# A fused linear-attention and token-mixing kernel: 128-token chunks on full 128-row operands with a block-diagonal state, whole-batch loads, and an explicit order that assigns every PSUM bank

## The chip, the cores and the metric

The kernel runs on one core of a Trainium2 chip. The metric is the device time of one execution in microseconds (us), as a median over several executions. A profile is a recording of one of them; its "span" is about 1.7 us shorter than the time of the same run (113.8 us against 115.53 us in a run of the kernel before). "Slow" here means over 1.5% above the fastest run of the same kernel.

## The reference, cut to what matters

```python
# q, k, v: (batch 4, heads 8, seq 768, head_dim 64), float32
gamma = 1.0 - 2.0 ** (-5.0 - np.arange(H))
for t in range(S):                                   # linear attention with decay
    state = gamma * state + einsum('bhd,bhe->bhde', k[:, :, t], v[:, :, t])
    y[:, :, t] = scale * einsum('bhd,bhde->bhe', q[:, :, t], state)
x = y as (B, S, 512)
wq, wk = x @ w_q, x @ w_k                            # 512 -> 64
W_tok = scale * einsum('bsd,btd->bst', wq, wk)
mixed = einsum('bst,btd->bsd', W_tok, x)
out = maximum(mixed, 0) @ w_out                      # (4, 768, 512) float32
```

Both kernels process it in 12 pairs of two 128-token chunks, three pairs to a batch. Two words are used throughout: a "filler" is a matmul on zeros whose result nobody reads, issued to keep TensorE busy; an "eviction" is a copy of a result from PSUM, where TensorE writes, to SBUF. The decay is folded into k and q when they are cast to bf16. Inside a chunk, scores are computed, masked and multiplied with v ("intra"); what came earlier enters through a 64x64 state per head ("inter"). The second half then works on the 256 tokens of a pair.

Of the kernel before, what the change touches and what calls it, by code (L numbers as in the profile page):

```python
# [9 lines left out]
FP32 = mybir.dt.float32  # L10
# [5 lines left out]

ORDER = """
fill.80 ck.0:V trk.0 cq.0:V ekT.0:A trq.0 cv.0:V fill.2 eqT.0:V
st.0 es.0.0:A sc.0.0 X.0 eat.0.0:V es.0.1:A sc.0.1 ck.1:P ia.0.0
eat.0.1:V cq.1:P Y.0 trk.1 fill.6 ekT.1:A ia.0.1 ex.0:V cv.1:P  # L20
trq.1 eqT.1:A xt.0 st.1 sc.1.0 exT.0:V ck.2:P es.1.0:A eat.1.0:V
X.1 es.1.1:A sc.1.1 cq.2:P trk.2 eat.1.1:V ia.1.0 ekT.2:V Y.1
ia.1.1 cv.2:A ex.1:V trq.2 st.2 fill.4 eqT.2:V xt.1 es.2.0:A
W:V sc.2.0 exT.1:A X.2 wqk.0 eat.2.0:V wqk.1 WO:A ew.0:V
sc.2.1 ew.1:V ia.2.0 eat.2.1:V ck.3:P Y.2 ia.2.1 ex.2:A cq.3:P
trk.3 xt.2 ekT.3:A fill.4 exT.2:V cv.3:A wqk.2 trq.3 ew.2:A
st.3 eqT.3:V zm.0 ck.4:P es.3.0:A ez.0:A X.3 sc.3.0 es.3.1:A
mx.0 eat.3.0:V r.0.1:A cq.4:P trk.4 r.0.0:A sc.3.1 ekT.4:A ia.3.0
eat.3.1:V mx.1 Y.3 r.1.0:A pj.0.0 cv.4:P r.1.1:A trq.4 fill.4
eo.0.0:A st.4 eqT.4:V ia.3.1 ck.5:P pj.0.1 ex.3:A es.4.0:V sc.4.0  # L30
eo.0.1:A X.4 eat.4.0:V xt.3 es.4.1:V cq.5:P trk.5 ekT.5:A exT.3:V
pj.1.0 sc.4.1 eo.1.0:A cv.5:P trq.5 eat.4.1:V ia.4.0 mx.2 eqT.5:A
YS.4 ia.4.1 es.5.0:A ck.6:P r.2.0:A ex.4:V wqk.3 trk.6 r.2.1:A
sc.5.0 pj.1.1 ew.3:A eat.5.0:V cq.6:P eo.1.1:A X.5 ekT.6:V ia.5.0
sc.5.1 cv.6:A xt.4 eat.5.1:V trq.6 pj.2.0 exT.4:A eqT.6:V ck.7:P
YS.5 eo.2.0:A sc.6.0 es.6.0:A ia.5.1 eat.6.0:V wqk.4 cq.7:P ex.5:A
pj.2.1 ew.4:A trk.7 eo.2.1:V xt.5 ekT.7:V sc.6.1 X.6 exT.5:V
cv.7:A eat.6.1:V trq.7 ia.6.0 eqT.7:A wqk.5 ck.8:P es.6.1:A sc.7.0
ew.5:V YS.6 eat.7.0:V es.7.0:A ia.6.1 zm.1 ex.6:A cq.8:P sc.7.1
ez.1:V X.7 eat.7.1:V trk.8 es.7.1:A xt.6 ekT.8:V cv.8:A ia.7.0  # L40
trq.8 exT.6:V Y.7 st.8 eqT.8:V mx.3 es.8.0:A ia.7.1 ck.9:P
r.3.1:A r.3.0:V sc.8.0 ex.7:V wqk.6 eat.8.0:V pj.3.0 ew.6:A cq.9:P
trk.9 eo.3.0:A pj.3.1 ekT.9:V X.8 eo.3.1:A cv.9:P mx.4 sc.8.1
r.4.0:A r.4.1:V trq.9 eat.8.1:V pj.4.0 eqT.9:A ck.10:P ia.8.0 eo.4.0:V
mx.5 YS.8 r.5.1:A r.5.0:V sc.9.0 ia.8.1 es.9.0:V pj.4.1 cq.10:P
ex.8:V trk.10 eo.4.1:A eat.9.0:V pj.5.0 ekT.10:A trq.10 cv.10:A eo.5.0:V
sc.9.1 X.9 eat.9.1:V ia.9.0 xt.8 ck.11:P xt.7 eqT.10:A exT.7:V
pj.5.1 exT.8:V wqk.7 es.9.1:V cq.11:P eo.5.1:A trk.11 ew.7:A wqk.8
YS.9 ew.8:V cv.11:P ekT.11:A sc.10.0 ia.9.1 es.10.0:A eat.10.0:V trq.11
ex.9:A zm.2 eqT.11:V X.10 ez.2:A sc.10.1 es.10.1:A ia.10.0 eat.10.1:V  # L50
mx.6 YS.10 r.6.0:A xt.9 es.11.0:A r.6.1:A sc.11.0 exT.9:V ia.10.1
mx.7 eat.11.0:V pj.6.0 r.7.0:A ex.10:V r.7.1:A wqk.9 eo.6.0:A pj.6.1
ew.9:A X.11 eo.6.1:A sc.11.1 ia.11.0 eat.11.1:V mx.8 pj.7.0 r.8.0:A
r.8.1:A Y.11 eo.7.0:V ia.11.1 pj.7.1 ex.11:A eo.7.1:A xt.10 xt.11
exT.10:V pj.8.0 exT.11:V wqk.10 eo.8.0:A wqk.11 ew.10:A pj.8.1 ew.11:A
zm.3 eo.8.1:A ez.3:A mx.9 r.9.0:A r.9.1:V mx.10 pj.9.0 r.10.1:A
r.10.0:V eo.9.0:V pj.9.1 mx.11 eo.9.1:A r.11.1:V r.11.0:A pj.10.0 eo.10.0:A
pj.10.1 eo.10.1:A pj.11.0 eo.11.0:A pj.11.1 eo.11.1:A
""".split()

STAGES = 6
# [3 lines left out]
def kernel(  # L65
# [16 lines left out]

# [5 lines left out]
    C = 128  # L88
    G = C // 2
    NP = S // (2 * C)  # L90
# [9 lines left out]
    def pool(name, bufs, **kw):  # L100
        return ctx.enter_context(tc.tile_pool(name=name, bufs=bufs, **kw))

    const_pool = pool("const", 1)
    stage_pool = pool("stage", STAGES)
    cast_pool = pool("cast", 3)
    qkt_pool = pool("qkt", 2)
    at_pool = pool("at", 2)
    s_pool = pool("s", 4)
    x_pool = pool("x", 6)
    xt_pool = pool("xt", 2)  # L110
    moe_pool = pool("moe", 6)
    relu_pool = pool("relu", 2)
    ost_pool = pool("ost", 7)
    PSUM = bass.MemoryType.PSUM
    at_psum = pool("at_psum", 1, space=PSUM)
    y_psum = pool("y_psum", 1, space=PSUM)
    s_psum = pool("s_psum", 1, space=PSUM)
    psum = pool("psum", 3, space=PSUM)

    pairs = [dict() for _ in range(NG)]  # L120
    state_ps = [None] * B
    z_sbs = [None] * B
    ENGINES = {"A": nc.scalar, "V": nc.vector, "P": nc.gpsimd}

    def copy(e, out, in_):
        if e == "A":
            return nc.scalar.copy(out=out, in_=in_)  # L127
        return ENGINES[e].tensor_copy(out=out, in_=in_)  # L128
# [6 lines left out]
    def load(name, p):  # L135
        src = {"k": k, "q": q, "v": v}[name]
        b, cp = divmod(p, NP)
        t = stage_pool.tile([128, H, 2, D], FP32, name=name + "_st")
        eng = nc.scalar if (name, p) == ("k", 0) else nc.sync
        eng.dma_start(  # L140
            out=t.rearrange("g h j d -> g h (j d)"),
            in_=src[b, :, cp * 2 * C : (cp + 1) * 2 * C, :].rearrange(
                "h (g j) d -> g h (j d)", j=2
            ),
        )
        pairs[p][name + "_st"] = t

    wq_stage = const_pool.tile([128, NDM, DH], FP32, name="wq_stage")
    wk_stage = const_pool.tile([128, NDM, DH], FP32, name="wk_stage")
    wout_stage = const_pool.tile([128, NDM, DM], FP32, name="wout_stage")  # L150
    for p in range(STAGES):
        for name in "kqv":
            load(name, p)
        if p == 2:
            nc.sync.dma_start(out=wq_stage, in_=moe_w_q.rearrange("(a p) h -> p a h", p=128))
            nc.sync.dma_start(out=wk_stage, in_=moe_w_k.rearrange("(a p) h -> p a h", p=128))
            nc.sync.dma_start(
                out=wout_stage, in_=moe_w_out.rearrange("(a p) m -> p a m", p=128)
            )

    def release(name, p):

        if p + STAGES < NG:
            load(name, p + STAGES)



    warm = const_pool.tile([128, 128], BF16, name="warm")
    nc.vector.memset(warm, 0.0)
    ln_g = const_pool.tile([128, NP, H, 2], FP32, name="ln_g")  # L170
    for h in range(H):
        nc.vector.memset(ln_g[:, :, h, :], math.log(1.0 - 2.0 ** (-5.0 - h)))
    tq = const_pool.tile([128, NP, H, 2], FP32, name="tq")
    nc.gpsimd.iota(
        tq,
        pattern=[[2 * C, NP], [0, H], [1, 2]],
# [4 lines left out]
    lq = const_pool.tile([128, NP, H, 2], FP32, name="lq")  # L181
    nc.vector.tensor_tensor(out=lq, in0=tq, in1=ln_g, op=ALU.mult)
    fq = const_pool.tile([128, NP, H, 2], FP32, name="fq")
    fk = const_pool.tile([128, NP, H, 2], FP32, name="fk")
    nc.scalar.activation(out=fk, in_=lq, func=ACT.Exp, scale=-1.0)
    nc.scalar.activation(out=fq, in_=lq, func=ACT.Exp)

    identity = const_pool.tile([128, 128], BF16, name="identity")
    make_identity(nc, identity)



    cmask = const_pool.tile([128, 1, 2, C], BF16, name="cmask")
    cmask_b = const_pool.tile([128, 1, 2, C], BF16, name="cmask_b")

    def masks():
        for t, base in ((cmask, 0), (cmask_b, C)):
            nc.gpsimd.memset(t, 1.0)
            for j in range(2):
                nc.gpsimd.affine_select(  # L200
                    out=t[:, :, j, :],
                    in_=t[:, :, j, :],
                    compare_op=ALU.is_ge,
                    fill=0.0,
                    base=base - j,
                    pattern=[[0, 1], [1, 2], [2, G]],
                    channel_multiplier=-2,
                )
        nc.gpsimd.tensor_copy(out=cmask[64:128], in_=cmask_b[64:128])

    masks()

    wq_sb = const_pool.tile([128, NDM, 2, DH], BF16, name="wq_sb")
    wk_sb = const_pool.tile([128, NDM, DH], BF16, name="wk_sb")
    wout_sb = const_pool.tile([128, NDM, DM], BF16, name="wout_sb")

    def W(e):
        copy(
            e,
            wq_sb,  # L220
            wq_stage[:, :, None, :].to_broadcast([128, NDM, 2, DH]),
        )
        if e == "A":
            nc.scalar.mul(out=wk_sb, in_=wk_stage, mul=float(wk_scale))
        else:
            ENGINES[e].tensor_scalar_mul(out=wk_sb, in0=wk_stage, scalar1=float(wk_scale))

    def WO(e):
        copy(e, wout_sb, wout_stage)



    fills = [0]

    def filled(dst):
        for i in range(fills[0]):
            if dst.dtype == BF16:
                nc.tensor.transpose(dst, warm, identity)
# [19 lines left out]
    def ck(e, p):  # L258
        decay(e, p, "k", fk)
# [348 lines left out]
```

## The kernel before: the parts that the change touches

k, q and v are loaded one pair at a time, each with two neighbouring tokens on one partition. In memory a token of one head is 64 float32, 256 bytes, so a partition reads runs of 512 bytes. This layout has a price: the 128 tokens of a chunk then lie on 64 partitions, and state and intra products work on half the rows.

```python
def load(name, p):
    ...
    t = stage_pool.tile([128, H, 2, D], FP32, name=name + "_st")
    eng.dma_start(
        out=t.rearrange("g h j d -> g h (j d)"),
        in_=src[b, :, cp * 2 * C : (cp + 1) * 2 * C, :].rearrange("h (g j) d -> g h (j d)", j=2),
    )

def release(name, p):            # called by the cast that read the buffer
    if p + STAGES < NG:          # STAGES = 6
        load(name, p + STAGES)

def sc(e, p, half):              # scores: 16 matmuls of 64x64 operands
    ...
    nc.tensor.matmul(out=ps[rows(c), x, hi, j, :], lhsT=st["kT"][rows(x), hp, j, c, :],
                     rhs=st["qT"][rows(x), hp, c, :], ...)

def state(p, c):                 # 64x64 per head, 16 matmuls a chunk
    ...
    yield dict(out=state_ps[b][rows(x), hp, :], lhsT=st["ks"][rows(c), hp, j, x, :],
               rhs=st["vs"][rows(c), hp, j, x, :], ...)

def X(e, p):                     # inter and state, interleaved so that tiles run side by side
    together(inter(p, 0), state(p, 1))
```

## Time and profile before

| | before |
|---|---|
| time, median of 3 (range) | 114.93 us (114.74 to 116.0) |
| span of the profile | 114.7 us |
| TensorE busy, share of the chain that ended last | 94.7 us (83%), 70% |
| ScalarE, VectorE, GpSimd busy | 60.3, 65.0, 49.7 us |
| load stream | about 290 GB/s; the last record of k, q or v ends at 75.9 us |

The prediction below shows the lines and how to read them. In short: busy time is per engine, "PEclk" is the granted TensorE clock in tenths, "GB/s" is what the DMA engines moved in each of 40 slices, and the chain of waits follows the execution back from its last instruction, naming at each step what had been waited for. TensorE carries most of the chain, and the load stream fills two thirds of the span.

### The profile page before, as it was taken

To read this page: it belongs to the slowest core of one execution; us is meant where nothing else is said; L and a number is where in the kernel's file an instruction comes from. 1 tells how busy PE (TensorE), PEld (TensorE's weight loads), DVE (VectorE), ACT (ScalarE), POOL (GpSimd) and SP (SyncE) were. 2 spreads that over 40 slices of the span, in tenths; PEclk is the share of its full clock that TensorE was granted. 3 is DMA by queue.
4 is the path that set the end of the run, shared out by engine and by line. 5 is a ranking of instruction groups with operands and counts; after the bars stand their busy time and mean duration, and the time that the engine had idled before them with its cause. 6 is when DMAs were issued, how large, how long until landed. Compare 5 with 4: busy or idle time off the path is not lost.

```text
span 114.7 us, 4693 instructions
## 1 busy us (share of the span) xinstructions
PE 94.7 (83%) x2118; PEld 69.5 (61%) x2132; DVE 65.0 (57%) x87; ACT 60.3 (53%) x94; POOL 49.7 (43%) x41
## 2 busy tenths in 40 slices
PE   3977596993789899997994949999999999978830
PEld 3976485781678567854783836556887665733410
DVE  1057846994122837776595749389868964416200
ACT  5004153472364975954955404365777768464640
POOL 7302949206669767866668885663000000000000
PEclk9999958999558999999999995899999999999998
DMA  1999999999999989999999999993421004422472
GB/s 45 305 290 294 292 284 245 328 319 293 294 287 268 286 244 257 296 276 285 277 297 295 285 288 349 325 407 136 189 119 70 6 0 189 183 87 96 183 278 91
DMA packets 40916, 26.77 MB, mean 233 GB/s; under 512 B 1856, under 2 KB 38720, under 8 KB 40896
## 3 DMA queue, kind: packets, MB, share of 16 engines
q1 hardware_dynamic: 39856, 25.96, 78.4%
q10 hardware_dynamic: 1040, 0.52, 1.7%
q8 instruction: 16, 0.26, 1.0%
q14 instruction: 4, 0.03, 0.1%
HBM read 20.19 MB, written 6.29 MB: 231 GB/s over the span
## 4 chain that ended last, share of the span: by engine, by line
PE 70%; DVE 10%; issue 8%; DMA 5%; ACT 3%; DVEq 0%; ACTq 0%
PE o_ps L533 19%; PE at_ps L311 8%; PE y_ps L417 6%; PE xt_ps L440 6%; PE wqk_ps L455 6%; DVE at_sb L324 6%; PE qtr_ps L294 6%; DMA k_st<-in_k_dram 5%; PE y_ps L380 5%; PE z_ps L487 3%; PE ktr_ps L280 3%; PE wqk_ps L465 3%; PE mx_ps L509 3%; PE state_ps L380 2%; DVE qs L248 1%
## 5 line engine op out<-in xcount | busy, mean ns | idle before, releaser
L324 DVE TENSOR_TENSOR at_sb<-at_ps,cmask 128x1024 bf16<-128x1024 f32 x24 | 29.3, 1222 | 10.8 <-PE at_ps L311 10.6
L248 POOL TENSOR_TENSOR ks<-k_st,fk 128x1024 bf16<-128x1024 f32 x11 | 20.9, 1902 | 22.3 <-DMA k_st<-in_k_dram 16.6
L533 PE MATMUL o_ps<-wout_sb,relu 128*128 128x512 bf16 x82 | 23.9, 389 | 1.2 <-ACT o_st L127 0.3
L248 POOL TENSOR_TENSOR qs<-q_st,fq 128x1024 bf16<-128x1024 f32 x11 | 20.9, 1902 | 2.6 <-DMA q_st<-in_q_dram 2.6
L127 ACT COPY o_st<-o_ps 128x512 f32<-128x512 f32 x19 | 11.2, 587 | 10.8 <-PE o_ps L533 10.5
L311 PE MATMUL at_ps<-qT,kT 64*64 64x128 bf16 x384 | 11.0, 226 | 5.2 <-issue 2.5
L533 PEld LDWEIGHTS <-relu 128*128 128x128 bf16 x96 | 8.4, 99 | 8.3 <-issue 1.7
L127 ACT COPY kT<-ktr_ps 128x1024 bf16<-128x1024 bf16 x7 | 7.1, 1014 | 9.4 <-PE ktr_ps L280 9.4
L524 ACT ACTIVATE relu<-mx_ps 128x512 bf16<-128x512 f32 x18 | 10.2, 598 | 3.3 <-PE mx_ps L509 2.6
L311 PEld LDWEIGHTS <-kT 64*64 64x64 bf16 x384 | 7.3, 108 | 7.8 <-issue 6.7
L127 ACT CAST s_sb<-state_ps 128x256 bf16<-128x256 f32 x16 | 6.0, 373 | 9.7 <-PE state_ps L380 9.6
L380 PE MATMUL y_ps<-s_sb,qT 64*64 64x64 bf16 x320 | 9.8, 197 | 1.0 <-DVE at_sb L324 1.0
L128 DVE COPY xT<-xt_ps 128x1024 bf16<-128x1024 bf16 x10 | 6.7, 686 | 6.7 <-PE xt_ps L440 6.7
L380 PE MATMUL state_ps<-vs,ks 64*64 64x64 bf16 x320 | 9.1, 197 | 1.6 <-issue 1.6
L380 PEld LDWEIGHTS <-qT 64*64 64x64 bf16 x320 | 7.4, 111 | 4.7 <-issue 2.7
L417 PE MATMUL y_ps<-vs,at_sb 64*128 64x64 bf16 x384 | 10.0, 193 | 0.3 <-DVE at_sb L324 0.2
L127 ACT CAST x_nat<-y_ps 128x1024 bf16<-128x1024 f32 x6 | 6.1, 1012 | 5.2 <-PE y_ps L417 5.1
L417 PEld LDWEIGHTS <-at_sb 64*128 64x128 bf16 x384 | 7.2, 96 | 2.6 <-DVE at_sb L324 0.5
L380 PEld LDWEIGHTS <-ks 64*64 64x64 bf16 x320 | 7.2, 111 | 2.5 <-issue 2.1
L294 PE MATMUL qtr_ps<-identity,qs 128*128 128x128 bf16 x96 | 8.2, 234 | 0.5 <-DVE qs L248 0.5
L526 DVE TENSOR_SCALAR relu<-mx_ps 128x512 bf16<-128x512 f32 x6 | 4.1, 691 | 7.5 <-PE mx_ps L509 7.5
L280 PE MATMUL ktr_ps<-identity,ks 128*128 128x128 bf16 x96 | 7.9, 229 | 0.6 <-DVE ks L248 0.6
(57 smaller groups left out, 136.1 us busy)
## 6 DMA issues: line engine op xcount, KB each, us to landing
q_st<-in_q_dram SPq DMA_DIRECT2D x12, 512.0 KB, 7.6
v_st<-in_v_dram SPq DMA_DIRECT2D x12, 512.0 KB, 7.6
k_st<-in_k_dram SPq DMA_DIRECT2D x11, 512.0 KB, 7.6
out_dram<-o_st SPq DMA_DIRECT2D x11, 512.0 KB, 2.7
wout_stage<-in_moe_w_out_dram SPq DMA_DIRECT2D x1, 1024.0 KB, 5.7
k_st<-in_k_dram ACTq DMA_DIRECT2D x1, 512.0 KB, 6.2
out_dram<-o_st SPq DMA_DIRECT2D x2, 256.0 KB, 2.9
wq_stage<-in_moe_w_q_dram SPq DMA_DIRECT2D x1, 128.0 KB, 5.7
```

What stands on the lines that cost most here:

```text
L127: return nc.scalar.copy(out=out, in_=in_)
L248: ENGINES[e].tensor_tensor(out=st[name + "s"].rearrange("p hp j x d -> p x (hp j) d"), in0=st[name + "_st"].rearrange("p (x hp) j d -> p x ...
L280: nc.tensor.transpose(ps[:, hp, j], st["ks"][:, hp, j], identity)
L294: nc.tensor.transpose(ps[:, hp, :, j, :], st["qs"][:, hp, j], identity)
L311: nc.tensor.matmul(out=ps[rows(c), x, hi, j, :], lhsT=st["kT"][rows(x), hp, j, c, :], rhs=st["qT"][rows(x), hp, c, :], start=(hi == 0 and ...
L324: st["eat", half] = ENGINES[e].tensor_tensor(out=st["at", half].rearrange("p x hi j t -> p (x hi) (j t)"), in0=st["at_ps", half].rearrange ...
L380: out.append(nc.tensor.matmul(skip_group_check=True, **mm))
L417: nc.tensor.matmul(out=st["y_ps"][:, c, x, hp, :], lhsT=st["at", half][rows(c), x, hi, j, :], rhs=st["vs"][rows(c), hp, j, x, :], start=(( ...
L440: nc.tensor.transpose(ps[:, a, c, :], st["x"][:, c, a * 128 : (a + 1) * 128], identity)
L455: nc.tensor.matmul(out=ps[:, 0 : 2 * C].rearrange("p (j c g) -> p j c g", j=2, c=2), lhsT=wq_sb[:, a].rearrange("p o h -> p (o h)"), rhs=s ...
L524: nc.scalar.activation(out=dst, in_=src, func=ACT.Relu)
L533: nc.tensor.matmul(out=ps, lhsT=st["relu"][:, a, j], rhs=wout_sb[:, a, :], start=(a == 0), stop=(a == NDM - 1),)
```

## The change

The intent is to use all 128 rows of TensorE. Chunk c of a pair is now one token per partition, so k and v of a chunk are full 128-row operands. Two heads share one 128x128 state product, of which only the two diagonal 64x64 blocks are kept (a mask on VectorE or two half copies on ScalarE); the block-diagonal state then serves two heads in one inter matmul. k, q and v are loaded a whole batch at a time with two buffers each. The order names the PSUM bank of every step. The core of the diff, with the regions of the order list and of unchanged helpers cut:

```diff
-    def load(name, p):
-        t = stage_pool.tile([128, H, 2, D], FP32, name=name + "_st")
-        ... "h (g j) d -> g h (j d)", j=2            # k, q and v: runs of 512 B
+    def load(name, b):
+        if name == "q":
+            t = buf("q_st", b % 2, [H, NP, 2, D], FP32)
+            ... "h (n p j) d -> p (h n) (j d)", p=128, j=2   # q: runs of 512 B
+        else:
+            t = buf(name + "_st", b % 2, [H, NCH, D], FP32)
+            nc.sync.dma_start(
+                out=t.rearrange("p h n d -> p (h n) d"),
+                in_=src[b].rearrange("h (n p) d -> p (h n) d", p=128),   # k, v: 256 B
+            )
 ...
     def release(name, p):
-        if p + STAGES < NG:
-            load(name, p + STAGES)
+        b = p // NP
+        casts[name, b] = casts.get((name, b), 0) + 1
+        if casts[name, b] == NP and b + 2 < B:
+            load(name, b + 2)
 ...
+    def sc(e, at, p, c):
+            for x in range(2):
+                nc.tensor.matmul(out=ps[:, x, hp, :], lhsT=st["kT"][rows(x), c, hp, :],
+                                 rhs=st["qT"][rows(x), c, hp, :], ...)
 ...
+    def st_(e, at, p, c):
+            nc.tensor.matmul(out=state_ps[:, hp, :],          # 128x128, two heads
+                lhsT=st["ks"][:, c, 2 * hp : 2 * hp + 2, :].rearrange("p x d -> p (x d)"),
+                rhs=st["vs"][:, c, 2 * hp : 2 * hp + 2, :].rearrange("p x d -> p (x d)"), ...)
 ...
+    def es(e, at, p, c):
+        if e == "V":
+            nc.vector.tensor_tensor(..., in0=state_ps, in1=dmask..., op=ALU.mult)
+        else:
+            for x in range(2):
+                copy(e, t[rows(x), :, x, :], state_ps[rows(x), :, x * 64 : x * 64 + 64])
 ...
+    singles = [psum.tile([128, 512], FP32, name=f"bank{i}_ps") for i in (4, 5, 6)]
+    state_ps = psum.tile([128, HP, 128], FP32, name="state_ps")
```

## The prediction

> **What bounds the kernel now.** I read the page first: busy shares, granted clock, DMA row, chain that ended last.
>
> ```profile
> PE 94.7 (83%) x2118; PEld 69.5 (61%) x2132; DVE 65.0 (57%) x87; ACT 60.3 (53%) x94; POOL 49.7 (43%) x41
> PEclk9999958999558999999999995899999999999998
> GB/s 45 305 290 294 292 284 245 328 319 293 294 287 268 286 244 257 296 276 285 277 297 295 285 288 349 325 407 136 189 119 70 6 0 189 183 87 96 183 278 91
> q8 instruction: 16, 0.26, 1.0%
> HBM read 20.19 MB, written 6.29 MB: 231 GB/s over the span
> PE 70%; DVE 10%; issue 8%; DMA 5%; ACT 3%; DVEq 0%; ACTq 0%
> ```
>
> TensorE carries 70% of the chain, and the loads run at about 290 GB/s until slice 27, that is until about 78 us: two streams of nearly equal length, TensorE being the longer. "issue" holds 8% of the chain. In the chain in order of time it sits in a few long pieces (start, length):
>
> ```profile
> 26.11 1.50 issue
> 51.41 0.96 issue
> 61.70 1.41 issue
> 66.86 1.62 issue
> ```
>
> These are waits of TensorE that name no releaser. The trace's packet records have fetches of 16 KB on the instruction queue beginning at 25.9, 50.3, 61.2 and 66.4 us, about 1.1 us each: TensorE ran out of instructions. That is 5.5 us here, and the clock row shows half speed in two spells later (29.1 to 35.9 and 70.0 to 73.5 us), about 5 us of work lost. What the steps cost, from the same chain (pieces that stand alone, at full clock):
>
> ```profile
> 44.25 0.45 PE ktr_ps L280 x8
> 46.80 0.22 PE mx_ps L509 x4
> 47.73 0.54 PE wqk_ps L455 x4
> 48.27 0.23 PE wqk_ps L465 x8
> 59.15 0.34 PE y_ps L417 x16
> 74.86 0.35 PE at_ps L311 x16
> 106.46 3.63 PE o_ps L533 x16
> ```
>
> So 56 ns for a 128-column transpose, 29 ns for 64 columns on full rows, about 215 ns for 512 columns. The timeline adds what the chain hides: the state and inter-chunk matmuls of 64x64 tiles run four at a time; the 32 of one step begin between 54.46 and 54.73 us, some 8.4 ns each. Reading that step as 32 times 23 ns would promise a large gain that isn't there.
>
> The evictions' prices, by line:
>
> ```profile
> L324 DVE TENSOR_TENSOR at_sb<-at_ps,cmask 128x1024 bf16<-128x1024 f32 x24 | 29.3, 1222 | 10.8 <-PE at_ps L311 10.6
> L248 POOL TENSOR_TENSOR ks<-k_st,fk 128x1024 bf16<-128x1024 f32 x11 | 20.9, 1902 | 22.3 <-DMA k_st<-in_k_dram 16.6
> L127 ACT CAST s_sb<-state_ps 128x256 bf16<-128x256 f32 x16 | 6.0, 373 | 9.7 <-PE state_ps L380 9.6
> ```
>
> **What the Trainium skill says.** "TensorE: Matmul & The Clock Gate", section "Wait — 56ns, not 53.3ns?", gives warm start-to-start times of 55.6 ns at 128 columns and 215.7 ns at 512; the trace agrees (56, 215). Its section "Part 3: Packing small matmuls — row/col tiling" says tiles at different array positions run at the same time; the trace agrees (8.4 ns above). So four 64x64 tiles are already full use of the array, and one 128x128 block-diagonal matmul does the same time's work on half zeros. "DMA: Bandwidth & Descriptors", sections "Specifications" and "Why small descriptors are slow (HBM only)", says line rate wants at least 512 B and that a 256 B descriptor carries 27% overhead. This case has 1,024 packets of 256 B (the wq and wk loads): median 18 ns each, against 29 for 512 B, so 24% more per byte. The trace agrees in size.
>
> **The change part by part.**
>
> Attention on TensorE, per chunk of 128 tokens. Scores: 16 matmuls of 64x64 by 128 columns (0.35 us) become 8 of 64x128 by 128 columns, paired in two row tiles and two banks. The mx step shows that pairing: 4 x 256 columns in 0.22 us. So 0.22 us, 24 times: -3.1 us. Intra-chunk product: 16 (0.34) become 8 on full rows at 29 ns, 0.23: -2.6 us. State and inter: 640 matmuls at 8.4 ns (5.4 us) become 160 of 128 columns at 56 ns (9.0): +3.6 us. The net is only -2 us. The rest of TensorE is unchanged: 36 blocks of transposes at 0.45 (16.2), 12 wqk at 0.77 (9.2), z 3.1, mx 12 x 0.25 (3.0), projections 24 x 0.87 (20.9): 52.4 us. After, attention adds 24 x (0.22 + 0.23) + 160 x 0.056 = 19.8: 72 us in total against 74 before. Fillers go from 100 to 194, nearly all before the first data.
>
> Instructions. TensorE's stream falls from 4,266 to 2,726 rows. At 0.26 MB for the old one, that is about 0.17 MB, 10 or 11 fetches in place of 16, and each instruction lasts longer, so the fetch has more time. I expect the fetch waits to fall from 5.5 to about 1.5 us, and one clock drop fewer: together -4 to -7 us.
>
> Loads. q keeps packets of 512 B. k and v now put one token on a partition: 256 B each, 6,144 per batch, 384 per DMA engine. At 290 GB/s a 512 B packet leaves every 28.2 ns (512 x 16 / 290), while its record lasts about 33: they overlap 1.17-fold. For 256 B: 18 / 1.17 = 15.4 ns. So k or v of a batch takes 5.9 us, q 192 x 28.2 = 5.4, a batch 17.2, four 68.9; wq and wk 1.0; wout 2.7 at the 389 GB/s it has now. From 2.2 us, and 0.6 for landing, the last v lands at about 75 us, three before today's end. Without the overlap (18 ns) it would be 83. The stores are issued behind all loads in the same queue and with six output buffers don't stop the work.
>
> Start. k of the whole first batch lands at 2.2 + 5.9 + 0.6 = 8.7 instead of 7.0, the cast takes 1.2, and 150 fillers (34 in the first 3 us, then 60 ns each) end at about 11. TensorE's real work begins at 11 against 8.4, and v only lands at 20. Some 5 us of work that today lies before 20 us moves behind it.
>
> Evictions. The state copy on ScalarE becomes two of 64 rows, and 373 ns depends on columns, not rows: 28 for 16, +4.5 us. Twenty half-size x copies at 0.59 replace six of 1.01: +5.6; three score copies +3; others leave (wout, copies of kT and qT). ScalarE ends near 66, VectorE near 73 (21 x 1.22 masks, 30 copies of 0.69, the rest as today). Both lie beside TensorE, but at 70% busy in-order engines make each other wait.
>
> Sum, path one: TensorE. The second batch's v lands at 41 on the same reckoning (20 + 1.0 + 5.9 + 2.7 + 5.4 + 5.9) and is cast by 42. By then the order has given TensorE about 20 of its 72 us of work. The 52 left, with 20% for waits and drains, take 62 (the old kernel's 68 us of work after 18.5 took 91.6, of which about 10 were fetches and clock: 1.2): 104.4. Then the last eviction and store: 110.1 to 114.7 in the chain, 4.6. That is 109.
>
> Path two: the last v. On ScalarE its cast stands ahead of the fourth pair's relus, so behind the landing at 75 come the cast 1.1, two relus 1.2, then 16 projections 13.8, 7 mx 1.5, attention of the last batch 4.5, xt, wqk, z and one trq 4.9: 24.7, with 8% for stalls 26.7 (today's last 25 us lose that much), and 4.6: 108.6. The two paths end together, so the order was made for such a load stream. I take 108.5.
>
> **The rivals.**
> (1) Packets of 256 B with a stride of 32 KB are slower than the small wq sample: for, those 1,024 packets never ran at length and the stream thinned out among them; against, the 150 fillers and the one-batch lead look sized for k landing near 9 us. At 18 ns path two gives 116.6: the gain is gone.
> (2) The gain is in the array: full 128-row operands as such. If the 64x64 steps cost 23 ns each, attention would fall by 11 us and the time to about 102. The overlapping starts in the timeline speak against it.
> (3) VectorE becomes the bound, 73 us of work in a window of 85: chains of score, mask, product stretch. That adds 3 to 5 us to path one: about 113.
> (4) Fetch waits don't fall, because they come from fetches queued behind a busy DMA and not from the count: +4, 112.5.
>
> **Range and chances.** Centre 108.5. The load rate gives 107 to 115, eviction coupling +4, a smoother TensorE -4. Eight in ten: 104 to 114.5. Faster by over 2% means under 112.6: 0.74. Within 2%: 0.18. Slower, over 117.2: 0.08, nearly all from rival 1.
>
> **What would show it.** The 256 B packets' rate: last v landing at 73 to 78 us and 260 to 290 GB/s until then; 83 would prove rival 1. TensorE's busy time little changed outside fillers, with about 1,320 matmuls. The "issue" pieces over 0.9 us falling from four to one or two, the instruction queue at 10 or 11 packets. ScalarE near 66 and VectorE near 73 us busy. The first transposes at about 11 us. The prediction is wrong if the chain shows TensorE waiting on loads beyond 80 us, or on masks by VectorE throughout.

## The result, and the profile after

The changed kernel took 125.52 us in the median of 4 runs (124.07 to 126.43, one of them slow), against 115.12 us for the kernel before in the same rounds. A ratio in this document is the mean time of one kernel's fast runs over that of the other's of the same rounds, so it isn't quite the ratio of the medians. Here it is 1.085, with a 95% interval of 1.072 to 1.098: the kernel became slower. The prediction said 108.5 us. The granted clock doesn't explain the loss: its mean is 0.959 in the profiled run, against 0.936 in that of the kernel before.

The page of the changed kernel (busy time per engine; busy tenths of TensorE, granted clock and GB/s in 40 slices of 3.1 us; the instruction queue; the chain that ended last by engine and by line; two groups of instructions with busy us, mean ns and idle time before them):

```profile
span 124.1 us, 3189 instructions
PE 99.0 (80%) x1362; PEld 73.3 (59%) x1362; DVE 74.5 (60%) x97; ACT 61.4 (49%) x112; POOL 53.7 (43%) x46
...
PE   6998464589975697499999387899399999999940
...
PEclk9999999968999999959999999999958999999999
...
GB/s 67 225 217 287 279 219 217 125 247 218 332 316 281 220 214 226 217 190 305 256 218 217 224 206 288 281 220 217 382 314 12 169 104 70 0 250 116 284 243 122
...
q8 instruction: 10, 0.16, 0.6%
...
SPq 58%; PE 23%; DMA 11%; issue 2%; ACT 2%; ACTq 0%
...
L282 POOL TENSOR_TENSOR ks<-k_st,fk 128x1024 bf16<-128x1024 f32 x10 | 20.8, 2100 | 20.2 <-DMA k_st<-in_k_dram 17.0
...
L138 ACT CAST s_sb<-state_ps 64x256 bf16<-64x256 f32 x28 | 10.3, 367 | 4.5 <-PE state_ps L418 4.2
```

Two things changed sides. TensorE fell from 70% to 23% of the chain, and the load queue with its transfers ("SPq" and "DMA") rose to 69%. The GB/s row alternates between about 220 and about 290, where the kernel before stood near 290 throughout; and the loads last until slice 29, about 88 us. That GpSimd waits 17.0 us for k is no sign of the change: it waited 16.6 us for it before.

The chain in order of time (start, length, what) is a list of load issues laid end to end, from the first microsecond until the last v lands. From 37.9 us on, without the pieces under 0.5 us:

```profile
37.91 8.01 SPq L159
46.39 7.64 SPq L153
54.48 3.12 SPq L159
58.07 8.59 SPq L159
67.12 6.70 SPq L153
74.27 14.17 DMA v_st<-in_v_dram
88.79 0.68 issue
89.47 0.60 ACT relu L539
90.11 0.77 PE bank_ps L330 x8
...
117.55 1.74 PE bank_ps L547 x8
119.31 0.58 ACT o L138
```

"SPq L159" is the queue busy with issuing a load of k or v, "L153" one of q. Most of these issues take five to nine microseconds, about what one load takes to land once it flows (7.25 us, worked out below), so I read them as the queue held up by the loads ahead: one nearly uninterrupted load stream. It ends at 74.27 + 14.17 = 88.44 us. From there to the end of the span it is 124.1 - 88.4 = 35.7 us.

Which loads run at which rate is seen in stretches of 5 us. The columns are the busy time of the five engines with the number of instructions, the granted clock, the DMA share and GB/s:

```profile
5.00:10.00 5.00, 5.00 (x92) 5.00 (x91) 0.00 (x0) 0.00 (x0) 0.00 (x0) 1.00 1.11 222
...
20.00:25.00 5.00, 2.68 (x52) 2.00 (x54) 4.89 (x5) 2.35 (x4) 1.78 (x3) 1.00 0.75 162
...
40.00:45.00 5.00, 3.91 (x37) 1.97 (x34) 2.68 (x5) 2.04 (x4) 3.39 (x2) 1.00 1.11 220
...
50.00:55.00 5.00, 3.73 (x44) 2.53 (x44) 2.36 (x2) 3.97 (x7) 0.86 (x1) 0.79 0.89 181
55.00:60.00 5.00, 5.00 (x76) 3.67 (x74) 3.58 (x4) 2.81 (x8) 3.84 (x3) 0.87 1.03 305
```

The stretches 5 to 10 and 40 to 45 us hold k or v, in runs of 256 B, and little else (in the first, the last half microsecond is q): 220 to 222 GB/s. The stretch 55 to 60 us is mostly q, in runs of 512 B: 305 GB/s. The kernel before, with runs of 512 B alone, had this stretch:

```profile
5.00:10.00 5.00, 3.90 (x66) 3.49 (x63) 2.93 (x3) 0.99 (x1) 0.00 (x0) 1.00 1.17 290
```

The DMA share is the time that the packet records took, as a share of 16 engines' time. It is above 1 because records overlap: 1.11-fold in the slow stretches, 1.17-fold in the kernel before. So the transfers weren't waiting for work; they were slower per byte. The trace's packet records say the same: over stretches of k and v alone the stream moves 217 GB/s, which is 256 x 16 / 217 = 18.9 ns for a run of 256 B on each of 16 engines, and 384 x 18.9 ns = 7.25 us for k or v of a batch. A record of k or v lasts 83.5 ns there and covers four runs, 20.9 ns each, which the overlap of 1.11 turns into 18.8. The stretches 20 to 25 and 50 to 55 us are two partial gaps, of (222 - 162) / 222 x 5 = 1.4 us and (220 - 181) / 220 x 5 = 0.9 us; the first is where the small wq and wk loads ran.

### The profile page after: what moved, and what is told of

Its sections match the earlier page's. It is cut to its first block, busy times and chain, and to the rows that moved or that the text cites. A ratio compares the mean times of both kernels' runs of the same rounds, so it can differ in the third digit from the quotient of the medians.

```text
span 124.1 us, 3189 instructions
## 1 busy us (share of the span) xinstructions
PE 99.0 (80%) x1362; PEld 73.3 (59%) x1362; DVE 74.5 (60%) x97; ACT 61.4 (49%) x112; POOL 53.7 (43%) x46
## 4 chain that ended last, share of the span: by engine, by line
SPq 58%; PE 23%; DMA 11%; issue 2%; ACT 2%; ACTq 0%
SPq L159 28%; SPq L153 18%; DMA v_st<-in_v_dram 11%; PE bank_ps L547 9%; SPq L171 7%; SPq L174 5%; PE duo_ps L547 3%; PE duo_ps L349 1%; PE bank_ps L526 1%; PE bank_ps L467 1%; PE state_ps L418 1%; PE bank_ps L390 1%; PE bank_ps L405 1%; ACT o L138 1%; ACT relu L539 1%
## 5 line engine op out<-in xcount | busy, mean ns | idle before, releaser
L282 POOL TENSOR_TENSOR ks<-k_st,fk 128x1024 bf16<-128x1024 f32 x10 | 20.8, 2100 | 20.2 <-DMA k_st<-in_k_dram 17.0
L365 DVE TENSOR_TENSOR at<-duo_ps,cmask 128x1024 bf16<-128x1024 f32 x21 | 25.1, 1217 | 6.3 <-PE duo_ps L349 6.2
L547 PE MATMUL bank_ps<-wout_sb,relu 128*128 128x512 bf16 x72 | 19.7, 403 | 0.1
L274 PE MATMUL bank_ps<-warm 128*128 128x128 bf16 x191 | 13.1, 238 | 1.0 <-DVE warm L190 1.0
L274 PEld LDWEIGHTS <-warm 128*128 128x128 bf16 x194 | 13.0, 109 | 1.1 <-DVE warm L190 1.0
L138 ACT CAST x<-bank_ps 128x512 bf16<-128x512 f32 x18 | 10.4, 589 | 4.5 <-PE bank_ps L405 4.2
L138 ACT CAST s_sb<-state_ps 64x256 bf16<-64x256 f32 x28 | 10.3, 367 | 4.5 <-PE state_ps L418 4.2
L349 PE MATMUL duo_ps<-qT,kT 64*128 64x128 bf16 x192 | 9.7, 232 | 2.5 <-ACT at L138 1.5
L418 PE MATMUL state_ps<-vs,ks 128*128 128x128 bf16 x80 | 8.6, 236 | 3.8 <-ACT vs L138 3.7
L138 ACT CAST vs<-v_st 128x1024 bf16<-128x1024 f32 x7 | 7.1, 1044 | 8.8 <-DMA v_st<-in_v_dram 8.8
L138 ACT COPY o<-bank_ps 128x512 f32<-128x512 f32 x13 | 7.6, 586 | 7.5 <-PE bank_ps L547 7.5
## 6 DMA issues: line engine op xcount, KB each, us to landing
wq_stage<-in_moe_w_q_dram SPq DMA_DIRECT2D x1, 128.0 KB, 11.1
wk_stage<-in_moe_w_k_dram SPq DMA_DIRECT2D x1, 128.0 KB, 3.2
```

The costliest lines, as they stand in the source:

```text
L138: nc.scalar.copy(out=out, in_=in_)
L274: nc.tensor.matmul(out=ps[:, 0:128], lhsT=warm, rhs=warm, start=True, stop=True)
L282: ENGINES[e].tensor_tensor(out=t, in0=staged[name, p // NP][shape].rearrange(order), in1=table.to_broadcast([128, 2, H, D]), op=ALU.mult,)
L349: nc.tensor.matmul(out=ps[:, x, hp, :], lhsT=st["kT"][rows(x), c, hp, :], rhs=st["qT"][rows(x), c, hp, :], start=(hp == 0), stop=(hp == HP ...
L365: nc.vector.tensor_tensor(out=t.rearrange("p x hp t -> p (x hp) t"), in0=ps.rearrange("p x hp t -> p (x hp) t"), in1=cmask.rearrange("p o ...
L418: nc.tensor.matmul(out=state_ps[:, hp, :], lhsT=st["ks"][:, c, 2 * hp : 2 * hp + 2, :].rearrange("p x d -> p (x d)"), rhs=st["vs"][:, c, 2 ...
```

## The experiments

The theory after reading the traces ("load theory"): runs of 256 B instead of 512 B for k and v make the stream 34% slower per byte (290 / 217), the last v lands late, and the rest follows. Its rivals: the new structure itself (waits among the engines, two state copies for one, bank assignments) costs the time; the distance between the runs costs it, not their length; a single queue limits the rate; the whole-batch loads cost it; or the order puts work in the wrong place behind the last v. Runs e1 to e4 shared a chip on which the kernel before took 115.92 us, runs e5 to e8 another with 114.59 us. Four kernels (e1, e2, e5, e8) read the wrong tokens: the same bytes and the same instructions, another assignment of tokens to partitions. Their outputs are wrong, which doesn't matter for the times.

### e1: the changed kernel with 512 B runs

```diff
-                out=t.rearrange("p h n d -> p (h n) d"),
-                in_=src[b].rearrange("h (n p) d -> p (h n) d", p=128),
+                out=t.rearrange("p h (n j) d -> p (h n) (j d)", j=2),
+                in_=src[b].rearrange("h (n p j) d -> p (h n) (j d)", p=128, j=2),
```

> Same kernel, but k and v are read in runs of 512 B as q is (the tokens land in the wrong places, so the result is wrong on purpose; bytes, instructions and order are unchanged). Load theory (runs of 256 B go at 217 GB/s and set when the last v lands; the end comes a fixed 35.7 us after that): k and v of a batch 5.4 us in place of 7.25, the last v at about 74 in place of 88.4, time 109 to 113 us. Structure theory (block-diagonal matmuls, split copies and the order itself cost the time; the loads are only seen waiting): time stays over 121 us.

Measured: 111.11 us (110.67 to 112.28), ratio to the kernel before 0.9645 (0.953 to 0.976). Span, GB/s in 40 slices and chain by engine:

```profile
span 109.2 us, 3180 instructions
...
GB/s 25 316 293 290 297 288 281 271 290 348 329 290 296 289 291 294 293 292 293 290 295 293 293 294 292 300 403 362 30 59 140 99 99 0 192 192 192 192 293 91
...
PE 57%; DVE 19%; DMA 12%; ACT 4%; issue 2%; SPq 1%; DVEq 0%; ACTq 0%
```

The row stays near 290, the last v has landed at about 72.5 us (its last packet record ends at 72.0; ScalarE casts a part of it at 74.7), and TensorE is back as the main piece of the chain. One access pattern, with every instruction of the four compute engines left as it was, takes the kernel from 8.5% slower than before to 3.6% faster. The load theory stands; the structure's instructions don't cost the time.

### e2: the kernel before with 256 B runs

```diff
+        if name != "q":
+            eng.dma_start(
+                out=t.rearrange("g h j d -> g (h j) d"),
+                in_=src[b].rearrange("h (n g) d -> g (h n) d", g=128)[:, cp * 16 : cp * 16 + 16, :],
+            )
+            ...
```

> The kernel before, with its k and v loads cut into runs of 256 B instead of 512 (wrong tokens on purpose; same bytes, same number of loads). Load theory: 12.6 MB at 217 instead of 290 GB/s take 14.6 us more, the last load lands at about 92 instead of 78, time 125 to 130 us. Structure theory: the old kernel is bound by TensorE and swallows it, time 115 to 118 us.

Measured: 123.96 us (123.43 to 124.82), ratio 1.074 (1.065 to 1.083).

```profile
span 123.1 us, 4697 instructions
...
GB/s 42 267 218 225 257 192 238 206 331 173 252 219 214 233 200 263 181 250 218 251 230 188 227 201 273 206 203 228 267 265 331 406 214 101 81 164 170 96 242 176
...
PE 42%; SPq 24%; DMA 18%; POOL 5%; issue 4%; ACT 3%; DVE 0%; POOLq 0%; ACTq 0%
```

The old structure with the new runs is as slow as the change was, within 1%. Its loads last until about slice 31, and queue and transfers take 42% of a chain in which they had 5%. The load theory expected 125 us or more, so it was a little too pessimistic: that its small loads in the order of need soften the loss is argued, not shown. The theory that the structure is at fault falls here a second time. Crossing the two experiments gives the worth of each part. With wide runs the new structure takes 0.9645 of the old one's time; with narrow runs 1.085 / 1.074 = 1.010.

### e3: v issued from a second queue

```diff
-            nc.sync.dma_start(
+            (nc.scalar if name == "v" else nc.sync).dma_start(
+    load("v", 0)            # behind the second exponential on ScalarE
-cv.2:A st.0.0 ...
+cv.2:A lv.1 st.0.0 ...     # and two more places in the order
...
```

> The changed kernel with the four v loads issued by ScalarE's queue, k and q still by SyncE's; correct result. If a DMA engine needs a fixed 18.9 ns for each run of 256 B whichever queue it comes from: the last load lands at 86 to 89, time 122 to 126 us. If two queues let an engine overlap packets (in the kernel before, the first microseconds with two queues ran at about 350 GB/s with runs of 512 B, against 290 later): last load at 70 to 76, time 108 to 115 us.

Measured: 129.72 us (129.36 to 129.88), ratio 1.123. A stretch with k and v alone, and the issue of the fourth v on ScalarE's queue:

```profile
5.00:10.00 5.00, 5.00 (x80) 5.00 (x79) 0.00 (x0) 0.00 (x0) 0.00 (x0) 1.00 1.11 217
```

```profile
55.62 0.02 ACT L159 MOVE_SHAPE v_st<-in_v_dram  x1
55.67 6.28 ACTq L159 DMA_DIRECT2D v_st<-in_v_dram  x1
61.99 0.58 ACT L138 COPY o<-duo_ps 128x512 f32<-128x512 f32 x1 [6.35 <-issue]
```

Two queues together move 217 GB/s, as one did. The limit isn't the queue. The run was slower than all expectations. I put that down to two things that the trace shows: the two queues share the DMA engines, so that the casts of the first batch's k began at 12.1 us instead of 10.7 and those of its q at 24.6 instead of 17.2, and ScalarE stood 6.3 us behind one issue. How much each costs was not tested.

### e4: the casts of the last v moved behind ready work

In the order list "cv" is a cast of v, "pj" a projection, "mx" the mixing before it, "eo" an output copy and "st" a state product; the number is the pair, the letter the engine. Only the order changed: the three casts of the fourth batch's v stand behind the projections of pairs 4 and 5 instead of ahead of them, so that ready work would fill the time before the landing.

```diff
-trk.11@5 ... cq.11:P cv.11:A trq.10@6 ... cv.10:P trq.11@5 cv.9:A ... pj.4.0@6 ... pj.5.1@2
+trk.11@5 ... cq.11:P trq.10@6 ... pj.4.0@6 ... pj.5.1@5 eo.5.1:A ... cv.11:A cv.10:P cv.9:A st.9.0
```

> The changed kernel with the order changed near its end only: the casts of the last v move behind the fourth and fifth pair's mixing and projections (four projections, two mx, their relus and copies, z of the third batch), which need no load; correct result. Load theory with a badly placed wait: TensorE fills its 2 to 4 us of idleness before the landing at 88.4, time 120 to 123 us. If TensorE has nothing to gain there: 124 to 127 us.

Measured: 128.85 us (128.0 to 130.06), ratio 1.113: a miss. Two stretches behind the landing, first of this run, then of the changed kernel:

```profile
95.00:100.00 5.00, 3.88 (x56) 3.25 (x56) 3.80 (x4) 2.75 (x6) 0.00 (x0) 0.66 0.20 80
100.00:105.00 5.00, 3.83 (x71) 3.27 (x71) 2.09 (x3) 3.92 (x10) 0.00 (x0) 1.00 0.00 0
```

```profile
95.00:100.00 5.00, 4.92 (x77) 3.43 (x72) 4.08 (x4) 4.64 (x11) 0.00 (x0) 1.00 0.28 108
100.00:105.00 5.00, 5.00 (x86) 3.93 (x84) 2.77 (x4) 4.16 (x10) 0.00 (x0) 1.00 0.27 108
```

The moved projections did their work earlier, but ScalarE's first cast of this v now ran at 93.7 us instead of 88.5, and the state chain behind it, one step waiting for the next across two engines, had little left to fill its gaps: TensorE is busy 3.9 of 5 us where it had been 4.9 and 5.0. So this wait was not badly placed: of the two orders, the change's own is the better for its tail. That no better one exists isn't shown (e7 has a shorter tail).

### e5: 256 B runs that lie near each other

In the changed kernel neighbouring runs of one partition lie 32 KB apart. Here they lie 512 B apart (every second token), with the same length.

```diff
-            nc.sync.dma_start(...)
+            for e in range(2):
+                nc.sync.dma_start(
+                    out=t.rearrange("p h n d -> p (h n) d")[:, 24 * e : 24 * e + 24],
+                    in_=src[b].rearrange("h s d -> (h s) d")
+                        .rearrange("(p i e) d -> p i e d", p=128, e=2)[:, :, e],
+                )
```

> The changed kernel with k and v still read in runs of 256 B, but from rows 512 B apart instead of 32 KB apart (each load as two, even and odd rows; wrong tokens on purpose). If the length of the run alone sets the rate (18.9 ns per 256 B): v of the last batch still lands at 86 to 89 us, time 122 to 127 us. If it is the 32 KB stride in memory: near 290 GB/s, landing near 74, time 109 to 114 us as in the run with wide k and v.

Measured: 125.62 us (125.1 to 126.18), ratio 1.096 (1.083 to 1.109). A stretch of k and v alone:

```profile
5.00:10.00 5.00, 5.00 (x76) 5.00 (x75) 0.00 (x0) 0.00 (x0) 0.00 (x0) 1.00 1.29 222
```

222 GB/s again, and the same time as the changed kernel. The length of the run sets the rate here, not the stride. Nor does it matter how the runs are recorded: k and v have one packet record for each run here, and one for four runs in the changed kernel. This answers half of the prediction's rival 1, which had blamed both together.

### e6: the changed order, loads by pair

The order and every step stay, but k and v come one DMA per chunk (256 KB) and q one per pair (512 KB), in the order in which the casts want them.

```diff
-            t = buf(name + "_st", b % 2, [H, NCH, D], FP32)
-            ... in_=src[b].rearrange("h (n p) d -> p (h n) d", p=128)
+            t = buf(name + "_st", p % 6, [2, H, D], FP32)
+            for c in range(2):
+                s0 = (cp * 2 + c) * C
+                nc.sync.dma_start(out=t[:, c], in_=src[b, :, s0 : s0 + C, :].rearrange("h p d -> p h d"))
...
```

> The changed kernel with its own order, but k, q and v loaded by pair of chunks instead of by whole batch (runs of 256 and 512 B as before; k and v one load per chunk); correct result. If the whole-batch loads cost as such: work starts 4 to 5 us earlier and the last casts 1 to 3 us earlier, time 120 to 123 us. If only the total bytes and run length matter: the last load lands at the same 87 to 89 us, time 124 to 127 us.

Measured: 122.04 us (120.59 to 124.62, two of four runs slow), ratio 1.056 (1.040 to 1.072). The result is correct. The issues of k with count, size and median us from issue to landing, and a stretch early on:

```profile
k_st<-in_k_dram SPq DMA_DIRECT2D x24, 256.0 KB, 5.0
```

```profile
5.00:10.00 5.00, 5.00 (x80) 5.00 (x79) 1.23 (x1) 0.00 (x0) 1.90 (x1) 1.00 1.32 226
```

The rate is what it was (226 against 222 GB/s; a fifth of the bytes is q in this stretch), so loads six times smaller lose nothing, and the first casts of VectorE and GpSimd already ran before 10 us, where the whole-batch kernel had its first one at 10.7 us. TensorE gained nothing from that at the start: its first transposes begin at 12.0 us in both, here behind the 150 fillers. At the other end, the last cast of v starts at 88.3 us instead of 90.4. The gain is (1.085 - 1.056) x 115 = 3.3 us by the ratios of two chips, whose intervals just touch; against e5, which shared e6's chip and loads whole batches in two halves, it is 125.6 - 120.9 = 4.8 us (fast runs). Whole-batch loads cost some 3 to 5 us here, and I don't claim it closer than that.

### e7 and e8: loads by pair in the order of need, with an order made for the measured rate

e7 loads k, q and v of pair 0, then of pair 1, and so on, puts the stores behind all loads, and has a new order list worked out from the measured durations and from 217 GB/s. It is correct. e8 is e7 with 512 B runs, and so wrong.

```diff
 ...
+    LOADS = """k0 q0 v0 k1 q1 v1 wqk k2 q2 v2 k3 q3 wout v3 k4 q4 v4 k5 q5 v5""".split()
     def release(name, p):
+        if p + 6 < NG:
+            load(name, p + 6)
 ...
```

> The changed kernel's steps with loads by pair, in the order of need (k, q, v of one pair, then the next), and a new order made for 217 GB/s loads, so that only the last pair's attention and the last batch's mixing follow the last load; correct result. Load theory: last load at 86 to 89 us, about 19 us of work and 4.5 us of copy and store after it, time 110 to 115 us, at or under the kernel before. If TensorE and evictions bind instead: over 118 us.

> The same as the run before, with k and v read in runs of 512 B (wrong tokens on purpose). Load theory: last load at 73 to 76, after that TensorE and the copies bind: 103 to 108 us. If the new order binds by itself: the same time as the run before within 2 us.

Measured: e7 116.73 us (115.54 to 118.11, two of four runs slow, the profiled one among them), ratio 1.0125 (0.997 to 1.028). e8 109.76 us (108.46 to 112.42, two of four slow), ratio 0.949 (0.935 to 0.963). Both are over what the load theory expected (110 to 115 and 103 to 108): the loads matter as it says, but the rest takes longer than I reckoned. The chains by engine, first of e7, then of e8:

```profile
PE 31%; DMA 23%; SPq 23%; DVE 5%; issue 5%; ACT 4%; POOL 4%; POOLq 0%; DVEq 0%
```

```profile
PE 50%; DVE 18%; SPq 12%; ACT 5%; issue 4%; DMA 4%; POOL 2%; DVEq 0%; POOLq 0%
```

With loads that arrive in the order of need, and an order that expects them when they come, the 128-row structure with its real 256 B runs comes within the noise of the kernel before, but not past it. How much of that is the order and how much the loads, e7 alone doesn't tell; e6, with the loads alone, is at 1.056. In its profiled run the last v was cast on GpSimd at 90.9 us and the end came 116.4 - 90.9 = 25.5 us later, 10 us less than in the changed kernel; queue and transfers still hold 46% of the chain. The same kernel with wide runs is 5% faster than before. No correct version that I ran was faster than the kernel before.

## Why the prediction was wrong

The direction was wrong, and one step failed: the size of the load term. The prediction took 18 ns for a packet of 256 B from the 1,024 packets of wq and wk, and divided it by the overlap of 1.17 that it had worked out for packets of 512 B: 15.4 ns, 5.9 us for k or v of a batch, the last v at 75 us.

- **The load term.** Measured: 18.9 ns for a run of 256 B, and so 7.25 us for k or v of a batch. Both halves of 18 / 1.17 were off: in the stream a run took 20.9 ns of its packet record, not 18, and records overlapped 1.11-fold, not 1.17. Eight such loads come 8 x 1.35 = 10.8 us later in sum. Two partial gaps in the stream (1.4 and 0.9 us, shown above) make 2.3 us more. Together 13.1 of the 13.4 us by which the last v was late (88.4 against 75). The overlap had been worked out for one packet size and was carried to another, and the 18 ns came from a sample too short to show a rate: the two loads are over in 2.6 us (18.2 to 20.8 us in the kernel before), and the stream falls to 92 GB/s within them. The prediction also took its 24% as agreeing in size with the 27% of the page; these are different things. The page's 27% is the overhead's part of one 256 B descriptor, not its price against 512 B (the last section works that out).
- **Rival 1.** It named the right cause, and the prediction gave it nearly all of its 8% for slower. It was undersized too: at 18 ns it put the last v at 83 and the time at 116.6. The mark that it set for itself ("83 would prove rival 1") was overrun by 5 us. Its second half, the stride of 32 KB, fell in e5.
- **The argument that weighed against it.** "The 150 fillers and the one-batch lead look sized for k landing near 9 us": k landed at 10.7. An order list that seems made for a rate is no measurement of that rate.
- **The tail.** The prediction's path two ran 108.6 - 75 = 33.6 us from the landing to the end; measured 35.7. A right mechanism, 2.1 us short. The v cast did stand ahead of the relus, and the projections did form the end.
- **The frame.** Both paths were added up on the axis of the span and then given as a time, which is about 1.8 us longer (125.87 against 124.1 in the profiled run of the changed kernel). So 13.4 of landing, 2.1 of tail and 1.8 of frame make 17.3 us, against 125.5 - 108.5 = 17.0 in the medians.
- **The gain in instructions** came in its signs: 10 fetches on the instruction queue, and no "issue" piece over 0.9 us in the chain. In e1, where TensorE has the chain again, "issue" is 2% of it, against 8% before. That those waits were fetches stays argued. On the time axis of the chain the four fetches begin at 25.3, 49.6, 60.5 and 65.8 us, some 0.6 earlier than the prediction says, so that each wait begins within 0.6 us of its fetch's end, and the other 12 fetches of the kernel before are followed by no such piece. The "one clock drop fewer" didn't come: both clock rows show three spells. 1,362 matmuls were recorded where about 1,320 were expected; outside the fillers TensorE's busy time hardly changed (86.3 and 85.4 us), as predicted.
- **The array.** Rival 2, a large gain from full rows, didn't show: e1, with the loads out of the way, gained 3.6% over the kernel before, and the prediction's own 108.5 would have been 5.6%. It stands as argued, not as shown, that full rows bring nothing by themselves, since no run isolates the array from the fetches.
- **Evictions and rival 3.** ScalarE was busy 61.4 us (66 expected), VectorE 74.5 (73 expected), and the state copy of 64 rows took 367 ns, as a copy of 128 rows had (373). In the changed kernel VectorE didn't become the bound. With the loads out of the way it holds 19% of the chain (e1), against 10% before, so rival 3 is not ruled out for that case.
- **The start.** The first transposes ran at 11.96 us, where 11 was expected. But VectorE's first two casts of k, reckoned at 1.2 us each, took 1.23 and 2.92 us, because GpSimd's ran between them; the last section shows the lines.
- **e1 as the counterfactual.** With runs of 512 B the last v landed at about 72.5 us, 2.5 us before the assumed 75, and the kernel took 111.1 us: 2.6 us above the prediction, inside its range. TensorE leads e1's chain, so it tests path one: 109 and the 1.8 of the frame make 110.8. That is close, but the loads were faster than assumed, so it doesn't show that each of the other terms is right.
- **Two readings.** The line shown for 512 columns (3.63 us for 16) gives 227 ns; the 215 fits other pieces of the same chain (0.86 us for 4). And the loads of the kernel before end at 75.9 us by their packet records, not at about 78, so the predicted 75 was one microsecond ahead of them and not three.

## What to carry to other kernels

When a change alters the length of the contiguous runs of a large load, that is a change of bandwidth, and its price must come from a stretch where such runs fill the stream, or from a run made for it; a packet's duration in a short, thinning sample doesn't give it. Before moving data to fill an array's rows, cross layout and load in two throwaway kernels with wrong results (new structure with old runs, old structure with new runs): e1 and e2 separated a gain of 3.6% from a loss of 7.4% in two small edits. And an order list is made for landing times: when they move by 13 us, the order has to be made again. With loads by pair (e7) that won back about what the loads had taken, no more.

## What the Trainium skill lacked or had wrong

- "DMA: Bandwidth & Descriptors", section "Why small descriptors are slow (HBM only)": its three-cycle account gives 11 cycles for 256 B and by the same sum 16 + 3 = 19 for 512 B, so (2 x 11) / 19 = 1.16 times the time per byte (an estimate from that page; its second cost, the descriptor metadata, is left out). Measured in sustained streams: 217 against 290 GB/s, 1.34 times. The section's direction holds, its size would have misled in the same way as the prediction's own 15.4 ns.
- The same page, section "Rules for kernel authors", asks for at least 1 MiB per DMA. Here loads of 256 KB moved 226 GB/s and loads of 1.5 MB 222 GB/s, and the large ones made the kernel some 3 to 5 us slower (e6), because, as I read it, a cast waits for a whole load. The rule doesn't mention that cost; another page, "Perfetto Trace Analysis", section "DMA Optimizations", says only that smaller pieces may let some start sooner, without a size.
- "SBUF — State Buffer", section "Who interferes with whom", is right and was overlooked in the prediction: it says that a VectorE instruction with two SBUF inputs and a GpSimd instruction that reads SBUF exclude each other for the whole instruction. The trace of the changed kernel agrees (the two views are of the line of the casts, VectorE before 11.8 us and all of 8 to 22 us; duration in ns as min/median/max, then first and last start):

```profile
L282 DVE TENSOR_TENSOR ks<-k_st,fk x1: 1227/1227/1227, 10.7 to 10.7; 128x1024 bf16<-128x1024 f32 x1
```

```profile
L282 DVE TENSOR_TENSOR ks<-k_st,fk x2: 1227/2076/2924, 10.7 to 11.8; 128x1024 bf16<-128x1024 f32 x2
...
L282 POOL TENSOR_TENSOR ks<-k_st,fk x1: 2908/2908/2908, 10.8 to 10.8; 128x1024 bf16<-128x1024 f32 x1
```

  VectorE's first cast started first and took its usual 1.23 us. GpSimd's, started less than 0.1 us later, took 2.91 us where it takes 1.90 alone (e6), and VectorE's second took 2.92 us. The excess, about 1.0 and 1.7 us, is close to the time for which the other engine's cast was still running (1.2 and 1.8 us), so I read it that each was recorded as running while it waited. The page doesn't say that the wait shows as busy time of the instruction, without an idle entry, which is how it is overlooked in a profile.
- "Runtime: NRT & Kernel Launch", section "Instruction fetch mechanics", calls the cost of crossing a 16 KiB block of instructions mostly hidden and gives no price for when it isn't. In the kernel before, 16 fetches of 16 KB took 0.9 to 1.7 us each, and four of them were followed by TensorE idling for 0.96 to 1.62 us with no releaser named; that the fetch caused it is argued.
